# A gated recurrence and an MLP on one core: Strassen products in float32 replaced by three products of 12-bit halves

## The chip, the core and the metric

The kernel runs on one core of a Trainium2 chip. The metric is the device time of one execution in microseconds (us). All inputs come from device memory and the result goes back there.

## What is computed

The inputs q, k, v and alpha are float32 with 4 batches, 8 heads, 768 positions and 48 features a head. The weights are stored as 64-bit floats.

```python
for t in range(S):
    state = alpha[:, :, t, :, None] * state + np.einsum('bhd,bhe->bhde', k[:, :, t], v[:, :, t])
    y[:, :, t] = np.einsum('bhd,bhde->bhe', q[:, :, t], state)
x = y.transpose(0, 2, 1, 3).reshape(B, S, H * D)          # 4 x 768 x 384
mu = mean(x); var = mean((x - mu) ** 2)
xn = (x - mu) / sqrt(var + 1e-06) * g_ln
out = x + maximum(xn @ w_ch1, 0.0) @ w_ch2                # 384 -> 1536 -> 384
```

## The kernel before

The 768 positions are cut into 6 chunks of 128, so there are 24 blocks (chunk c, batch b) of 128 tokens. `attention(c, b)` (L298) takes one block from its loads to the normalised x, transposed for the MLP: logarithm of alpha and running sums (L317, L320, L407), scaled k and q (L327, L329), their transposition on TensorE in chunks 0 and 1 (L355) and by DVE and DMA from chunk 2 on (L366, L372, L379), masked scores (L397 in chunk 0, L405 later, L411 and L417), the state (L432, L441, L445, and the multiplication by the gates on POOL, L447), the outputs (L458, L463, L467), x, its mean and variance (L493, L496, L513), xn (L519, L523) and its transposition, on TensorE in chunks 0 to 3 (L530, L532), by DVE and DMA in chunks 4 and 5 (L536, L540, L543). From chunk 4 on (`split`, L387) the scores of the last head pair go to another buffer.

The weights come in 12 pieces of 768 KB, six of w_ch1 and six of w_ch2. `round_weights` (L209) turns each from 64-bit to float32 with integer operations on DVE (L219, L221, L223, L229), one activation (L227) and a multiplication on DVE (L233 with the gain g_ln, or L236).

The MLP of chunk 0 is plain: 12 hidden tiles of 128 for each half of the batches (`hidden`, L567 on TensorE, L570 on ACT), then 12 products a block (`project`, L579). From chunk 1 on it is made of fast matrix products in the manner of Strassen. The first layer is cut 3 x 3 x 2 and takes 15 products in place of 18 (`hidden_product`, L842, matmul in L857, 4 tiles of 128 x 256 a product and chunk). The sums that go into them are made on DVE (`combine_first`, L786, once; `combine_x`, L814, per chunk), and the results are put together on DVE, ACT and POOL (L865 to L900). `relus` (L903) rectifies in place. The second layer is cut 4 x 3 x 2 and takes 20 products in place of 24 (`product`, L676, matmul in L683, 4 matmuls of 128 x 192 a product and chunk), with sums by `combine_weights` (L625) and `combine_hidden` (L654, L670) and results by L693, L696 and, on POOL, L699.

PSUM has 6 banks under the tag "bank" and two for the state. All operands are float32.

Nothing reorders the work: every part is a Python generator, and the string `ORDER` says, letter by letter, whose next step is recorded. Each engine runs its instructions in that order and waits for semaphores. All transfers are issued from SyncE (SP), one queue.

Of the kernel before, what the change touches and what calls it, by code (L numbers as in the profile page):

```python
# [14 lines left out]
INT64 = mybir.dt.int64  # L15
AFT = mybir.ActivationFunctionType
AOP = mybir.AluOpType
# [4 lines left out]
X_BY_DMA = 4  # L22
SPLIT = 4
AHEAD = 2
G = 32
SCORES = ((0, 0), (0, 1), (1, 0), (1, 1), (3, 0), (2, 0), (3, 1), (2, 1))

ORDER = (
    "bacabcadaacbcaadbcadabcababbebaccbadbaaBbccaedcbceAeeaaacbfecfBcdafddeaedbdeafae"
    "bcdccbfgadhAdcgCcdbebeebfhggdfgbfffbCdcgfgecdfchgdfhgabcddchdhAiiegjhacehedhhjfg"
    "biAdfidAeBhBijffYYiCjZZYYifZYlZCgjYDlYYjjZZYBZYgDieEgDgDjZZekEhZYGZgZigZGeeYgYgg"
    "fZYEhfGfkChihiYFYijfgEhgkhFZYhgYfghijgkFeZZlGZShfZYHlhHfYFYZeZHelYiZgllPmZkJIgJk"
    "PeiYjJIflHeSZIQgkIlYSjiPkffennSQlOKjLSnSjmSQhKnSjLnKPkiljnhSQnLkkjkWknkShOmPhkhl"
    "kOOhWlmmphmQmkmXjWQnXjlSQjPmkilXSXkP2OXWjXQjkjW2iXoSWX2oWX22Pi2mnol1j1mom2omSpoo"
    "l1XSpk2oW2m112p1m2pm11m1W211pp12O122r22jnn21lpnmnjSml1riOn2l12Rl111kqS1m21W1Rkp2"  # L40
    "o21mUXpq1mU2rUrnmj1rl2Rno2oomqonrormpokO1rNM2Mipin1op1ionoqUM2qp2W12RkMmNqiMoRtk"
    "UrpkqNM1NoMliMlNUMMNMNMKNqMlNorMWrnmtltNRMsqppMWNMriMMMpNlsqqqnoqttNttMtMsXMMssM"
    "sMNMNMX1oXXppMvstM2MXMMNMsppXoMXoqMsMMXM1nqqv11Xq1trMq2tqX21rn12v1r2ur2r222rvsqs"
    "svsu1rs1nuvvt2s11ss11p22rtsvosn2uropuXru222221uts212stnU1211u1121222Op1Rp2tRU21R"
    "Us1pXqU11x2tO2MM1vwMUM12xuRvu1vurNNNNwtOuuMwRxvNtxRNutwwMM2MOwNXwMNuXMMtNM1rMMMw"
    "qtXMMMxNUNxtMMsNMMMxXxMtXtrMMqMNrMXNvutMMwNuMMMNMMMxMLMOM11vvuq2X2O2wMus1wX11222"
    "2r2Xt1222w22utsqxvw2x2ww1vx21sX12121xwvq2O2x2w111u1uvU121w12s1wuRvx12U11J1q21R1U"
    "OvRxU121wMMu2xxsRNMw2NNMRM1MUNN2MMuUMqXN1MrNNRMNvMXNXMMMM2MMMxNM1uNXMMNMNMOXMXMv"
    "MMXOMMMXxNxwxMMvNMMMMMXMx21w1x222212v12w222x122w2212X11UX2212121121121wx111MU11X"
    "2RR2v1211212211R1URU211XOUM2XNRX1MX1RM2MXN2MXNXNMXXMXMMMN111U1MN1M1122MNM1MM2MM1"  # L50
    "11NNN121O11NM1MM21N1112N1122M1MMM12MM12N222M22M2RM1M2N22MM2MU1ON2M22M2UURR22RNNM"
    "MNM1MMOMRMNMUUM2ONMNNNMO2MMMUMNMMMMMRMMNNMMMNMNMMNMMMMMMMMNMNMMMMMMM"
# [4 lines left out]
def kernel(  # L57
# [17 lines left out]

# [10 lines left out]
    NJ = DF // P  # L104
    assert S % P == 0 and H % 2 == 0 and D <= 64 and DM % P == 0 and DF % P == 0
# [3 lines left out]
    raw = ctx.enter_context(tc.tile_pool(name="raw", bufs=B // 2))  # L109
    stage = ctx.enter_context(tc.tile_pool(name="stage", bufs=STAGED))  # L110
# [4 lines left out]

    nc.scalar.preload_act_table_set("natural_log_exp_and_others")

    HS = P // 2
    halves = [slice(HS * s, HS * s + HS) for s in range(2)]

    raws = {}

    def load(c, m, names):

        bs = range(2 * m, 2 * m + 2)
        rows = slice(c * P, (c + 1) * P)
        for n, src in (("a", alpha), ("k", k), ("q", q)):
            if n in names:
                t = raw.tile([P, 2, 2, NP, D], FP32, name=f"r{n}", tag="in", bufs=7)
                step = 1 if n == "a" and c == 0 else 2  # L130
                for i in range(0, 2, step):
                    nc.sync.dma_start(  # L132
                        t[:, i:i + step].rearrange("t b i p d -> t b (i p d)"),
                        src[bs.start + i:bs.start + i + step, rows].rearrange("b t h d -> t b (h d)"))
                raws.update({(n, c, b): t[:, b - bs.start] for b in bs})
        if "v" in names:
            vn = raw.tile([P, 2, 2, NP, D], FP32, name="vn", tag="vn")
            nc.sync.dma_start(vn.rearrange("t b i p d -> t b (i p d)"),
                              v[bs.start:bs.stop, rows].rearrange("b t h d -> t b (h d)"))
            vx = None  # L140
            if c:


                vx = raw.tile([P, 2, NP, D], FP32, name="vx", tag="vx")
                src = v[bs.start:bs.stop, rows].rearrange("b (s t) h d -> s t b (h d)", s=2)
                parts = ((0, 0, NP, NP), (1, 0, NP, 0))
                if c >= SPLIT:
                    parts = ((0, 0, NP, NP - 1), (1, 0, NP - 1, 0), (1, NP - 1, 1, H - 1))
                for h, to, n, at in parts:
                    nc.sync.dma_start(  # L150
                        vx[halves[h]].rearrange("t b p d -> t b (p d)")[:, :, to * D:(to + n) * D],
                        src[1 - h, :, :, at * D:(at + n) * D])
            for b in bs:
                raws["v", c, b] = vn[:, b - bs.start], vx[:, b - bs.start] if c else None

    lone = {}

    def load_one(n):

        c, b = divmod(n, B)  # L160
        for n, src in (("a", alpha), ("k", k), ("q", q)):
            if n not in lone:
                lone[n] = raw.tile([P, 2, 2, NP, D], FP32, name=f"r{n}", tag="in", bufs=7)
            t = raws[n, c, b] = lone[n][:, b % 2]
            rows = src[b, c * P:(c + 1) * P]
            nc.sync.dma_start(t.rearrange("t i p d -> t (i p d)"),
                              rows.rearrange("t h d -> t (h d)"))
# [11 lines left out]
    for m in range(B // 2):  # L179
        load(0, m, "a")  # L180

    w1 = cpool.tile([P, NJ // 2, NF, 2 * P], FP32, name="w1")
    w2 = cpool.tile([P, NJ, DM], FP32, name="w2")
    small = cpool.tile([P, 2 * NF + 3], FP32, name="small")
    g_col, eps, least = small[:, :NF], small[:, NF:NF + 1], small[:, NF + 1:NF + 2]
    g_part, zero_col = small[:, NF + 2:2 * NF + 2], small[:, 2 * NF + 2:]
# [3 lines left out]
    pieces = []  # L190
    for i in range(NJ // 2):
        cs, js = slice(2 * i * P, 2 * (i + 1) * P), slice(2 * i, 2 * (i + 1))
        pieces.append((w1[:, i], w1_src[:, :, cs]))
        pieces.append((w2[:, js], w2_src[:, js]))
    pieces = pieces[::2] + pieces[1::2]
    staged = {}

    def load_weights(i):
        if i >= len(pieces):
            return  # L200
        dst, src = pieces[i]
        if src.dtype != FP32:
            dst = staged[i] = stage.tile(list(dst.shape), INT64, name="ws", tag="ws")
        nc.sync.dma_start(dst, src)
        if i == 0:
            with nc.allow_non_contiguous_dma(reason="one small column load"):
                nc.sync.dma_start(g_col, g_ln.rearrange("(f p) -> p f", p=P))

    def round_weights(i):  # L209

        dst, _ = pieces[i]
        ws = staged.pop(i)
# [9 lines left out]
        if i == 0:  # L225
            nc.scalar.mul(g_part, g_col, 2.0 ** -20)
# [12 lines left out]
    def take_weights(i):  # L239
        if i < STAGED:  # L240
            load_weights(i)
            yield
# [726 lines left out]
```

## Time and profile before

| | us |
|---|---|
| time, median of 3 runs (lowest to highest) | 421.62 (420.76 to 421.73) |
| span of the profiled execution, first to last instruction | 418.9 |
| TensorE (PE) busy | 409.0 |
| VectorE (DVE) busy | 351.4 |
| ScalarE (ACT) busy | 178.0 |
| GpSimd (POOL) busy | 153.2 |

The profiled execution has no time of its own beside its span; what lies around the span is taken as the difference to the median, 2.7 us. In the profile PE stands for matmuls and PEld for weight loads, which overlap them. L12 is line 12 of the kernel; a group names what is written and what is read (out<-in) and its shape. A matmul's record includes the way through the array, so records that follow each other overlap, and their spacing is read from the chain of waits, where each piece is counted from the end of the one before.

### The profile page before, as it was taken

The page shows a single profiled execution, that of the slowest core. Times are in us where ns is not written, and L with a number is a line of the kernel's source. Part 1 is how long each engine was busy: PE and PEld are TensorE (multiplying, and loading weights), DVE is VectorE, ACT ScalarE, POOL GpSimd, SP SyncE. Part 2 cuts the span into 40 slices and gives each one's busy share as a digit, 9 for nine tenths or more (in the row PEclk, how much of TensorE's full clock was granted, in tenths as well). Part 3 has the DMA queues.
Part 4 walks back from the last instruction along what each step waited for, and adds up shares of the span by engine and source line. Part 5 has one row for each costly group of instructions (what it writes and reads, how often), then busy time and mean ns, then how long its engine had stood idle before and what let it go on. Part 6 is the DMA issues. An engine that isn't in the chain of part 4 may idle for free.

```text
span 418.9 us, 11553 instructions
## 1 busy us (share of the span) xinstructions
PE 409.0 (98%) x4608; PEld 360.9 (86%) x4608; DVE 351.4 (84%) x713; ACT 178.0 (42%) x440; POOL 153.2 (37%) x169
## 2 busy tenths in 40 slices
PE   6998999999999999999999999999999999999996
PEld 4787888766678889998889999889998899999996
DVE  3999999999999989996888996688876767977873
ACT  5498456724243496414546612364313242014110
POOL 3011000003203990043395033493152940499123
PEclk9999999999999999999999999999999999999999
DMA  7998889987778778587784546433035200001201
GB/s 247 325 297 246 206 201 293 287 194 181 145 221 176 200 167 185 128 195 178 146 215 70 130 105 166 88 95 77 0 114 104 67 1 2 0 20 38 94 20 56
DMA packets 133741, 59.52 MB, mean 142 GB/s; under 512 B 90764, under 2 KB 129804, under 8 KB 133688
## 3 DMA queue, kind: packets, MB, share of 16 engines
q1 hardware_dynamic: 133688, 58.79, 55.1%
q8 instruction: 36, 0.59, 0.6%
q14 instruction: 17, 0.14, 0.1%
HBM read 42.17 MB, written 16.61 MB: 140 GB/s over the span
## 4 chain that ended last, share of the span: by engine, by line
PE 89%; DVE 4%; ACT 2%; DMA 2%; issue 1%; SPq 1%; POOL 0%; POOLq 0%; DVEq 0%
PE hps L857 31%; PE ops L683 30%; PE ops L579 8%; PE hps L567 8%; PE aps L405 3%; PE yps L463 3%; PE yps L467 2%; PE sums L432 2%; DMA rq<-in_q_dram 2%; PE xps L530 1%; PE tps L355 1%; PE aps L397 1%; PE lps L407 1%; SPq L132 1%; DVE w L221 0%
## 5 line engine op out<-in xcount | busy, mean ns | idle before, releaser
L699 POOL TENSOR_TENSOR ob<-ob,u 128x192 f32<-128x192 f32 x40 | 26.3, 668 | 64.5 <-DVE ob L696 48.3
L857 PE MATMUL hps<-sum,w 128*128 128x256 f32 x192 | 46.3, 381 | 0.0
L907 ACT ACTIVATE hT<-hT 128x512 f32<-128x512 f32 x48 | 28.8, 624 | 34.9 <-POOL hT L879 18.5
L447 POOL TENSOR_TENSOR mid<-mid,gate 112x192 f32<-112x192 f32 x20 | 11.4, 568 | 80.0 <-DVE mid L445 33.3
L683 PE MATMUL ops<-w,hT 128*128 128x192 f32 x224 | 40.5, 327 | 0.0
L857 PEld LDWEIGHTS hps<-sum,w 128*128 128x128 f32 x192 | 36.1, 190 | 5.0
L683 PEld LDWEIGHTS ops<-w,hT 128*128 128x128 f32 x224 | 37.1, 190 | 0.7 <-issue 0.2
L857 PE MATMUL hps<-xT,w 128*128 128x256 f32 x136 | 34.0, 380 | 0.0
L579 PE MATMUL ops<-w,hT 128*128 128x384 f32 x96 | 33.0, 491 | 0.0
L567 PE MATMUL hps<-xT,w 128*128 128x256 f32 x144 | 32.5, 382 | 0.0
L567 PEld LDWEIGHTS hps<-xT,w 128*128 128x128 f32 x144 | 27.0, 190 | 4.2
L683 PE MATMUL ops<-ws,sum 128*128 128x192 f32 x160 | 28.7, 327 | 0.0
L857 PEld LDWEIGHTS hps<-xT,w 128*128 128x128 f32 x136 | 25.5, 190 | 3.1
L683 PEld LDWEIGHTS ops<-ws,sum 128*128 128x128 f32 x160 | 26.5, 190 | 0.3
L579 PEld LDWEIGHTS ops<-w,hT 128*128 128x128 f32 x96 | 17.6, 190 | 10.7 <-DVE w L236 0.3
L693 DVE TENSOR_TENSOR ob<-ops,ob 128x192 f32<-128x192 f32 x50 | 17.3, 353 | 10.6 <-PE ops L683 6.5
L447 POOL TENSOR_TENSOR st<-st,gate 112x192 f32<-112x192 f32 x16 | 11.7, 729 | 37.3 <-DVE st L445 25.9
L683 PE MATMUL ops<-ws,hT 128*128 128x192 f32 x128 | 23.6, 328 | 0.0
L463 PEld LDWEIGHTS yps<-st,qT 48*64 48x64 f32 x320 | 19.9, 134 | 4.0 <-issue 2.0
L467 PE MATMUL yps<-vx,at 64*64 64x48 f32 x320 | 22.7, 219 | 0.0
L463 PE MATMUL yps<-st,qT 48*64 48x48 f32 x320 | 22.0, 220 | 0.6 <-ACT x L493 0.6
L405 PEld LDWEIGHTS aps<-qT,kT 48*64 48x64 f32 x576 | 19.0, 134 | 4.1 <-issue 0.8
(255 smaller groups left out, 1134.2 us busy)
## 6 DMA issues: line engine op xcount, KB each, us to landing
ws<-in_moe_w_ch_dram SPq DMA_DIRECT2D x12, 768.0 KB, 5.9
td<-tr SPq DMA_DIRECT2D x64, 96.0 KB, 3.1
vn<-in_v_dram SPq DMA_DIRECT2D x12, 384.0 KB, 4.3
kept<-x SPq DMA_DIRECT2D x20, 192.0 KB, 3.0
ob<-kept SPq DMA_DIRECT2D x20, 192.0 KB, 3.1
out_dram<-ob SPq DMA_DIRECT2D x19, 192.0 KB, 1.9
ra<-in_alpha_dram SPq DMA_DIRECT2D x16, 192.0 KB, 2.6
kT<-td SPq DMA_DIRECT2D x32, 96.0 KB, 4.2
```

What stands on the lines that cost most here:

```text
L405: nc.tensor.matmul(to, kT[rs, p, s], qT[rs, p, s], start=True, stop=True)
L432: nc.tensor.matmul(up[h, p], qk_of(c, b)[ts, 1, p, i, :h.stop - h.start], vn[ts, i, p], start=True, stop=True)
L447: nc.gpsimd.tensor_mul(new, new, by)
L463: nc.tensor.matmul(yps[i][halves[s], i, p], qT[rs, p, s], (now, mid)[s][rs, p], start=True, stop=r != i)
L467: nc.tensor.matmul(yps[r][halves[s], i, p], at[halves[r], p, s], by, start=r != i, stop=True)
L567: nc.tensor.matmul(hps, w1[:, j // 2, f, j % 2 * P:][:, :P], xT_of[0][:, f, bs], start=(f == 0), stop=(f == NF - 1))
L579: nc.tensor.matmul(ops_of[b], hT_of[c][:, j, b], w2[:, j], start=(j == 0), stop=(j == NJ - 1))
L683: nc.tensor.matmul(acc, lhs[:, j], rhs[:, j], start=(j == 0), stop=(j == NT - 1))
L693: nc.vector.tensor_add(x, acc, x)
L699: getattr(nc.gpsimd, f"tensor_{op}")(x, x, y)
L857: nc.tensor.matmul(acc[:, i], w, b, start=True, stop=True)
L907: nc.scalar.activation(out=x, in_=x, func=AFT.Relu)
```

## The change

In place of the fast products, the MLP from chunk 1 on splits each operand into a high and a low part of 12 bits: h = round((1 - 2^-13) w), l = w - h. With d = h - 2^12 l on the weights' side and 2^-12 h - l on the other, three products give the whole: a sum of h h and l l in one accumulation, times (1 + 2^-12), minus the product of the differences. All operands of these matmuls are float32r. Chunk 0 keeps its float32 products.

- **Weights.** `take_weights` scales on ACT and multiplies on POOL what L233 and L236 did on DVE. `split_weights` makes three tiles a piece: two activations on ACT, two subtractions on POOL.
- **x.** All chunks are transposed on TensorE. Two activations (ACT), a subtraction on DVE and one on POOL make the three parts, per block.
- **First layer.** For each half-chunk (two batches) and each two hidden tiles: 6 matmuls for the difference, 12 for the sum, 256 columns each, in two banks. Then a copy (ACT), a scaled sum (DVE), two rectified copies (ACT), the low part (DVE) and the difference (POOL). The middle of this chain has two buffers, the hidden tiles have one set for all half-chunks.
- **Second layer.** Per block 12 matmuls of 384 columns for j 0 to 5, 12 for j 6 to 11, 12 for the difference; two DVE operations add them to x.
- **Loads** of alpha, k, q and v are by block. The number of DMAs is 397, before 390.
- **ORDER** is new throughout.

The added functions, cut to their core (numbers on the left are the changed kernel's lines):

```diff
+    # take_weights, after the integer operations (175 to 185)
+            act(out=lo, in_=lo, func=AFT.Relu, scale=8.0, bias=least)
+                for f in range(NF):
+                    act(out=dst[:, f], in_=dst[:, f], func=AFT.Copy, scale=g_part[:, f:f + 1])
+            stt(out=hi, in0=hi, scalar=-(1 << 31), in1=lo, op0=AOP.bitwise_and,
+                op1=AOP.bitwise_or)
+            nc.gpsimd.tensor_mul(dst, dst, hi.bitcast(FP32))
+    def split_weights(i):                                            # 192 to 200
+        whole, _, high, low, diff = pieces[i]
+        act(out=rd(high), in_=whole, func=AFT.Copy, scale=1 - LOW / 2)
+        nc.gpsimd.tensor_sub(rd(low), whole, high)
+        act(out=rd(low), in_=low, func=AFT.Copy, scale=1 / LOW)
+        nc.gpsimd.tensor_sub(rd(diff), high, low)
...
+        act(out=rd(xh), in_=xps, func=AFT.Copy, scale=1 - LOW / 2)   # 460 to 465, attention
+        act(out=rd(xs), in_=xps, func=AFT.Copy, scale=LOW * (1 - LOW / 2))
+        nc.vector.tensor_sub(rd(xl), xps, xh)
+        nc.gpsimd.tensor_sub(rd(xs), xs, xl)
...
+    def first_products():                                            # 520 and 526
+        for m in PAIRS:
+            for t in range(NT):
+                for i in range(2):
+                    for f in range(NF):
+                        nc.tensor.matmul(b[:, i], rd(wj[i * NF + f][2]), rd(xv[f][2]),
+                                         start=(f == 0), stop=(f == NF - 1))
+                yield
+                for i in range(2):
+                    for f in range(NF):
+                        for e in range(2):
+                            nc.tensor.matmul(a[:, i], rd(wj[i * NF + f][e]), rd(xv[f][e]),
+                                             start=(f == 0 and e == 0),
+                                             stop=(f == NF - 1 and e == 1))
+    # the hidden step, in five generators (540 to 570)
+                act(out=z_of(t), in_=acc_of.pop(("b", m, t)), func=AFT.Copy, scale=-1.0)
+                stt(out=z_of(t), in0=acc_of.pop(("a", m, t)), scalar=1 + LOW, in1=z_of(t),
+                    op0=AOP.mult, op1=AOP.add)
+                act(out=rd(high), in_=z_of(t), func=AFT.Relu, scale=1 - LOW / 2)
+                act(out=rd(diff), in_=z_of(t), func=AFT.Relu, scale=LOW * (1 - LOW / 2))
+                stt(out=rd(low), in0=z_of(t), scalar=0.0, in1=high, op0=AOP.max,
+                    op1=AOP.subtract)
+                nc.gpsimd.tensor_sub(rd(diff), diff, low)
+    def second_products():                                           # 586
+                    js = range(NJ) if part == 2 else range(part * NT, part * NT + NT)
+                    for j in js:
+                        of = pieces[NT + j // 2][2:]
+                        for k, x in ((2, hs),) if part == 2 else ((0, hh), (1, hl)):
+                            nc.tensor.matmul(a, rd(x[:, j, i]), rd(of[k][:, j % 2]),
+                                             start=j == 0 and k != 1, stop=j == NJ - 1 and k != 0)
+    def results():                                                   # 595 and 598
+                stt(out=ob, in0=acc_of.pop(("a", c, b)), scalar=1 + LOW, in1=ob,
+                    op0=AOP.mult, op1=AOP.add)
+                nc.vector.tensor_sub(ob, ob, acc_of.pop(("b", c, b)))
+                send(c, b)
-    combine_weights, combine_hidden, product, combine_first, combine_x, hidden_product, relus
```

More of the change, by code (lines that the diff above doesn't have):

```diff
@@ L15 @@
 INT64 = mybir.dt.int64
+F32R = mybir.dt.float32r
 AFT = mybir.ActivationFunctionType
@@ L118 @@
     HS = P // 2
     halves = [slice(HS * s, HS * s + HS) for s in range(2)]
[L121 to L154, printed above, removed]
@@ L178, with at_first @@
         nc.gpsimd.tensor_copy(out=consts[h, 2 * P:], in_=tri[h, h])
[L179 to L183, printed above, removed]
+    def at_first(name, then):
+        return [cpool.tile([P, then[0] * then[1]], FP32, name=n, tag=name, bufs=1)
+                for n in ("early_" + name, name)]
+    w1h, w1l = (cpool.tile([P, NT, NF, 2 * P], FP32, name=n) for n in ("w1h", "w1l"))
+    early, w2h = at_first("w2h", (NJ, DM))
```

861 lines of the change are left out of this document (295 added, 566 removed).

## The prediction

> **What bounds the kernel now.** I read the page first: its totals, its slices and the chain.
>
> ```profile
> span 418.9 us, 11553 instructions
> ...
> PE 409.0 (98%) x4608; PEld 360.9 (86%) x4608; DVE 351.4 (84%) x713; ACT 178.0 (42%) x440; POOL 153.2 (37%) x169
> ...
> PE   6998999999999999999999999999999999999996
> ...
> DVE  3999999999999989996888996688876767977873
> ...
> PEclk9999999999999999999999999999999999999999
> ...
> PE 89%; DVE 4%; ACT 2%; DMA 2%; issue 1%; SPq 1%; POOL 0%; POOLq 0%; DVEq 0%
> PE hps L857 31%; PE ops L683 30%; PE ops L579 8%; PE hps L567 8%; PE aps L405 3%; PE yps L463 3%; PE yps L467 2%; PE sums L432 2%; DMA rq<-in_q_dram 2%; PE xps L530 1%; PE tps L355 1%; PE aps L397 1%; PE lps L407 1%; SPq L132 1%; DVE w L221 0%
> ```
>
> PE is busy in every slice but the first and the last, its clock is full throughout, and 61% of the chain is the two Strassen products (L857, L683). A busy PE is not yet a PE at its peak, so I asked for its work by stage, and for the chain in order of time, where back-to-back records show their true spacing.
>
> ```profile
> 0.00:40.00 40.00, 34.04 (x573) 27.90 (x574) 32.23 (x72) 28.39 (x73) 6.40 (x15) 1.00 0.96 286
> 40.00:410.00 370.00, 369.28 (x4003) 327.57 (x4002) 316.15 (x635) 149.26 (x367) 143.89 (x149) 1.00 0.52 128
> 410.00:419.00 9.00, 5.68 (x35) 5.38 (x34) 2.99 (x7) 0.32 (x1) 2.87 (x5) 1.00 0.19 66
> ```
> ```profile
> 39.75 11.85 PE hps L567 x54
> ...
> 80.59 2.58 PE ops L579 x8
> ...
> 84.47 0.33 PE xps L530 x3
> ...
> 300.61 13.00 PE ops L683 x80
> 313.61 24.17 PE hps L857 x112
> ```
>
> (The columns of the first are PE, PEld, DVE, ACT and POOL busy.) From 40 to 410 us PE is never free, and no other engine is as full. A record of 256 columns takes 24.17/112 = 0.2158 us, one of 192 columns 13.00/80 = 0.1625, one of 384 columns 2.58/8 = 0.3225: all are 0.833 ns a column and 2.5 ns. So the price of the MLP is columns times records, and the change is read on PE.
>
> **The change, part by part.** A float32 product is two records here:
>
> ```profile
> L567 PE MATMUL hps<-xT,w 128*128 128x256 f32 x144 | 32.5, 382 | 0.0
> ...
> L857 PEld LDWEIGHTS hps<-xT,w 128*128 128x128 f32 x136 | 25.5, 190 | 3.1
> ...
> L530 PEld LDWEIGHTS xps<-consts,xn 128*128 128x128 f32 x48 | 5.7, 141 | 3.1 <-ACT small L226 1.8 <-issue 0.4
> ```
>
> L567 stands for 24 tiles of 3 products, 72, and has 144 records. *Removed:* L857 makes 15 products x 4 tiles x 5 chunks = 300 matmuls, 600 records, x 0.2158 = 129.5 us; L683 makes 20 x 4 x 5 = 400, 800 records, x 0.1625 = 130.0 us. Together 259.5 us.
>
> *Added:* 10 half-chunks x 12 tiles x 3 blocks x 3 terms = 1080 matmuls of 256 columns, and 20 token blocks x 12 x 3 = 720 of 384 columns. Both are 276,480 columns. No row shows a float32r matmul. From above it costs what a record costs now, 0.2158 and 0.3225 us; the transposes, one record each, also take 0.33/3 = 0.110 us for 128 columns. From below it costs half the stream: 256 x 0.4167 + 2.5 = 109.2 ns and 162.5 ns. I take the lower end: two records are needed now because one operand comes in two parts, and by the same arithmetic the other part of each record's time goes to the two parts of the other operand; with both cut to 12 bits neither is left. Then the sum is 1080 x 0.1092 + 720 x 0.1625 = 117.9 + 117.0 = 234.9 us, **24.6 us less** than 259.5. The upper end gives 465.3 us, 205.8 more.
>
> The Trainium skill ("FP8 and Floating Point Precision", TensorE Precision Notes) says the same of the passes: true FP32 is four, and a reduced FP32 reads four bytes and truncates to FP22. By that sentence the sum is the lower end; no run so far shows it.
>
> The weights must be hidden as well. A load of 128 float32 columns is modelled at 190 ns, and the transposes' at 141; the 215.8 ns cycle of L857 hides it. At 109 ns there is less room. The nearest row with a load and a stream of equal length is the score product of chunk 0, in two row groups that run beside each other:
>
> ```profile
> L397 PE MATMUL aps<-qT,kT 48*128 48x128 f32 x18 | 1.4, 291 | 0.0
> ```
>
> These are the records that start between 12.6 and 13.6 us: 9 in each group, one per 111 ns, for a stream of 128 x 0.833 = 107 ns. So a load as long as the stream adds some 2.5 ns, 2.7 us over 1080 records. I count nothing for it and keep 2.7 for the range. The margin is narrow: 24.6 us over 1800 records is **13.7 ns a record**.
>
> *Chunks 4 and 5 of x* were turned by DVE and DMA (L536, L540, L543) and now go through PE: 8 x 3 transposes x 0.110 = **+2.6 us**. Attention's other PE work stays in number: scores, sums and outputs only lose the special case of the last head pair (L387).
>
> *DVE* loses the Strassen sums, and *ACT and POOL* gain:
>
> ```profile
> L907 ACT ACTIVATE hT<-hT 128x512 f32<-128x512 f32 x48 | 28.8, 624 | 34.9 <-POOL hT L879 18.5 <-POOL hT L895 8.2 <-DVE hT L889 4.4
> ...
> L873 ACT COPY u<-hps 128x512 f32<-128x512 f32 x8 | 4.7, 584 | 12.9 <-PE hps L857 9.9 <-issue 3.1
> ```
> ```profile
> L869 DVE TENSOR_TENSOR hT<-hps,hT 128x512 f32<-128x512 f32 x8 | 5.5, 689 | 1.9 <-PE hps L857 1.7
> ```
> ```profile
> L883 POOL TENSOR_TENSOR hT<-hT 128x512 f32<-128x512 f32 x8 | 11.1, 1391 | 0.6
> ...
> L879 POOL TENSOR_TENSOR hT<-hT,u 128x512 f32<-128x512 f32 x8 | 10.2, 1280 | 6.3 <-DVE hT L878 6.2
> ```
>
> Each of 60 hidden steps (two tiles of 256 columns) needs on ACT one copy from PSUM and two rectifiers, 0.58 + 2 x 0.62 = 1.8 us; on DVE two passes, 1.4 us; on POOL one subtraction, 1.3 to 1.4 us. PE has 18 x 0.109 + 12 x 0.1625 = 3.9 us of work for the same step, and more with attention. Averaged over the MLP these engines are under half full, so I cost this chain at nothing, hidden behind the other products and attention, with two exceptions.
>
> (1) **The splitting of the weights.** POOL gains for each of 12 pieces one product and two subtractions of 768 columns; 768/512 of 1.28 us is 1.9 us. The built order on POOL puts, between the first hidden subtraction and the point where the last three pieces of w2 have their low halves, 3 hidden steps more and 10 weight subtractions, with four small operations of attention: 4 x 1.3 + 10 x 1.9 + 3.3 = 27.5 us, and up to the last difference one hidden step and 2 weight subtractions more, 33 us in all. On PE the same stretch holds the rest of the first half-chunk, part of the next one, attention and the first two parts of a w2 product, 28 us. That leaves 33 - 28 = **+5.0 us** of PE waiting. On ACT this stretch has 8 x 1.8 us of hidden steps, 12 scalings of the weights and attention's share, some 34 us, so it ends no earlier. Nothing on PE stands behind it but the same products, which wait with it; lower bound 0, if PE comes there late for other reasons, upper bound 15, if all of ACT's excess adds.
>
> (2) **The last half-chunk**, when attention is over. The low half of its last tiles comes after DVE 0.7, ACT 1.2, DVE 0.7 and four hand-overs, 3 us; one part of a w2 product, 12 x 0.1625 = 1.95 us, can run meanwhile. **+1.3 us.** The end after the last matmul stays:
>
> ```profile
> 414.22 1.46 PE L683 MATMUL ops<-w,at 128*128 128x192 f32 x8
> ...
> 415.96 0.36 DVE L693 TENSOR_TENSOR ob<-ops,ob 128x192 f32<-128x192 f32 x1 [1.12 <-POOL ob L699]
> ```
>
> PE ends at 415.7 now, 3.2 us before the end of the span; afterwards it is one DVE pass (0.56 for 384 columns) and one DMA again.
>
> *Start.* The first w1 matmul stands at 39.75 us with DVE full until then. In the new order less of chunk 1 comes before it, so it should start about 8 us earlier, but with about 9 us less of PE work done: no gain, give or take 4. *SP* has 397 transfers for 390: 40 go with the turning of x, and the loads are cut by batch. DMA is 52% full in the long stage, so I count nothing; what waits behind a late transfer on SP is the next load of the same kind, one block ahead.
>
> *Sum:* 418.9 - 24.6 + 2.6 + 5.0 + 1.3 = 403.2 us of span. The median of the runs is 421.6, 2.7 above this span: 403.2 + 2.7 = **405.9 us**.
>
> **The rivals.**
> *Clean:* the order hides the splitting, and the start gains 4: 405.9 - 5.0 - 1.3 - 4 = 395.6 (391 to 397). For it: PE is full for 370 us today with DVE at 85%, so an order can hide a near-full engine. Against: POOL and ACT both exceed PE in one stretch. 0.12.
> *Starved:* the five-engine chain of a hidden step (PE, ACT, DVE, ACT, DVE, POOL) has two buffers for its middle, and every half-chunk must wait until the one before has read the hidden tiles. One exposed hand-over of 1 to 2 us in each of 10 half-chunks, and the 15 us in the stretch above, give 413 to 435. It ends slower than before from 16 us of waiting beyond my 6.3. For it: 60 such chains are new; against: twice the time on PE for each. 0.20.
> *A dear record, slower:* the single-pass record isn't half the old one. It decides from (24.6 - 2.6 - 5.0 - 1.3)/1800 = 8.7 ns a record. At the transposes' 0.86 ns a column the time is 405.9 + 465.3 - 234.9 = 636 us; if only the weights' load binds the 256-column ones at 150 ns, 405.9 + 1080 x 0.041 = 450 us. For it: every float32 row streams at 0.83; against: the operands' halves. Here the change would not do what it says. 0.11.
> *Loads not hidden at all:* each full-array record pays its load of some 107 ns (as in L397) ahead of its stream: 405.9 + 1800 x 0.107 = 599 us. In L857 this is excluded: 0.2158 us is the stream alone. 0.02. The Trainium skill ("TensorE: Matmul & The Clock Gate", Part 3, The mechanism) states that LDWEIGHTS overlaps matmuls in flight only when the row group differs, which speaks for this rival; L857, all on full rows, disagrees by 107 ns a record.
>
> **How the numbers follow.** Forecast 405.9, its own range 397 to 413, 0.55; clean 0.12; starved 0.20; dear record 0.11; unhidden loads 0.02. A measurement can tell about 0.3%, 1.3 us, from no change. Starved lies for 0.08 below 420.3, 0.03 within, 0.09 above. Faster: 0.55 + 0.12 + 0.08 = 0.75; same 0.03; slower 0.09 + 0.13 = 0.22. For 8 in 10, the range takes the forecast, two thirds of clean and most of starved: 393 to 428.
>
> **What would show it.** Records of the w1 products 109 to 112 ns apart and of the w2 products 162 to 163; 1800 of them; PE waiting for POOL or ACT between the first w1 product of chunk 1 and its first w2 product, 4 to 8 us, and little after. Wrong: a spacing above 118 ns; PE free for over 1 us in most half-chunks; a first w1 matmul after 36 us.

## The result, and the profile after

The changed kernel takes **444.25 us** (median of 4 runs, 442.81 to 444.90) against 421.19 (420.45 to 421.73) of the kernel before on the same chip: 1.0555 times, 95% interval 1.0528 to 1.0582. The forecast was 405.9 us, with a range of 393 to 428. The profiled execution has a span of 442.6 us, 23.7 more than before.

The page of the changed kernel: totals, slices and chain.

```profile
span 442.6 us, 12334 instructions
...
PE 415.9 (94%) x5032; PEld 377.9 (85%) x5032; DVE 280.8 (63%) x428; ACT 261.9 (59%) x578; POOL 198.8 (45%) x165
...
PE   7799796999995899999799999999999999999996
...
POOL 2043645675469961731711905334518326153170
PEclk9989899599998699999999999999999999999999
...
PE 82%; DVE 8%; ACT 4%; issue 2%; DMA 2%; SPq 1%; POOL 1%; DVEq 0%
```

PE now has holes, all but one in the first 14 slices (to 155 us), and beside them its granted clock is down. The same by stretches (columns as in the prediction: PE, PEld, DVE, ACT, POOL busy, then the clock):

```profile
40.00:80.00 40.00, 33.31 (x359) 26.87 (x359) 35.51 (x35) 27.62 (x61) 22.05 (x14) 0.91 0.55 165
80.00:120.00 40.00, 40.00 (x284) 25.50 (x283) 22.60 (x29) 18.64 (x41) 24.06 (x17) 0.92 0.46 128
120.00:160.00 40.00, 32.26 (x426) 30.69 (x425) 28.76 (x33) 29.45 (x56) 34.41 (x22) 0.87 0.43 98
160.00:442.00 282.00, 276.17 (x3598) 267.04 (x3596) 161.98 (x273) 158.17 (x354) 109.45 (x100) 1.00 0.47 116
```

From 160 us on PE is full again at full clock. Its four longest waits, from the view of waits (the first three end before 160 us, the fourth lies at 211 us):

```profile
PE hpb L520 <- POOL xs L465: 7.0, 1, 7.0
PE hps L483 <- DVE at L366: 3.5, 1, 3.5
PE hps L483 <- DVE early_w2h L293: 2.5, 1, 2.5
PE opa L586 <- DVE at L546: 2.4, 1, 2.4
```

A second finding is in the chain in order of time, in stretches where nothing waits:

```profile
152.84 0.68 PE hpb L520 x6
153.52 1.36 PE hpa L526 x12
...
161.00 2.08 PE opb L586 x12
163.08 2.08 PE opa L586 x12
```

A record of 256 columns takes 1.36/12 = 0.1133 us, one of 384 columns 2.08/12 = 0.1733; I had put 109.2 and 162.5 ns. That alone is 1080 x 4.1 + 720 x 10.8 ns = 12.3 us.

To see where PE's time went I gave each record the time to the next record's start, took out waits over 0.3 us, and summed by line:

| PE, us | before | after | difference |
|---|---|---|---|
| MLP products of chunks 1 to 5 | 263.0 | 259.0 | -4.0 |
| MLP products of chunk 0 | 63.7 | 67.8 | +4.1 |
| attention and transposes | 81.0 | 86.9 | +5.9 |
| waits over 0.3 us | 6.6 | 23.8 | +17.2 |
| first to last record | 414.2 | 437.6 | +23.4 |

(The lines are rounded, and add up to 23.2.)

Of 24.6 us that the products should have saved, 4.0 arrived; and PE waits 17.2 us more. The two lines that hold most of it are different questions, so I split the time at one point, the first w2 product of chunk 1, from the view of its line:

```profile
L586 PE MATMUL opa<-w2h,hid x240: 333/334/446, 156.6 to 436.5; 128*128 128x384 f32 x120
...
L586 PE MATMUL opb<-ws,hid x240: 331/334/423, 160.8 to 438.7; 128*128 128x384 f32 x120
```

**The start stretch is 156.6 us, the rest 438.7 - 156.6 = 282.1 us**, and only 3.2 us of the waits lie in the rest. Below, these two figures are those of each run's profiled execution, not medians.

Why DVE is named in the waits can be read from its groups, of the kernel before and of the changed one (mean ns after the comma):

```profile
L221 DVE SCALAR_TENSOR_TENSOR w<-ws,w 128x768 f32<-128x768 uint32 x12 | 11.5, 959 | 0.4
...
L329 DVE TENSOR_TENSOR qk<-rq,eq 128x384 f32<-128x384 f32 x20 | 11.4, 569 | 0.4 <-DMA rq<-in_q_dram 0.4
```
```profile
L546 DVE SCALAR_TENSOR_TENSOR at<-hpa,at 128x512 f32<-128x512 f32 x60 | 40.9, 687 | 31.9 <-PE hpa L526 24.7 <-ACT at L540 3.8 <-ACT lps L287 1.3
L169 DVE SCALAR_TENSOR_TENSOR w<-early_w2l,w 128x768 f32<-128x768 uint32 x12 | 23.1, 1924 | 0.4
L295 DVE TENSOR_TENSOR qk<-qk,eq 128x384 f32<-128x384 f32 x16 | 18.8, 1176 | 0.0
...
L171 DVE TENSOR_SCALAR early_w2l<-early_w2l 128x768 int32<-128x768 int32 x12 | 10.4, 868 | 0.4
```

The first two of the kernel before take twice as long in the changed one (L221, now L169: 959 to 1924 ns; L329, now L295: 569 to 1176), while L546, which reads PSUM, has 687. L171, with one input from SBUF, has 868 here and 578 in run 1 below, where POOL has less to do. The timeline ahead of the 7.0 us wait, of POOL and of DVE, shows how:

```profile
134.76 1.86 POOL L200 TENSOR_TENSOR ws<-w2h,w2l 128x768 fp32r<-128x768 f32 x1
136.57 0.51 POOL L417 TENSOR_TENSOR st<-st,gate 112x192 f32<-112x192 f32 x1
137.03 1.84 POOL L196 TENSOR_TENSOR w2l<-w,w2h 128x768 fp32r<-128x768 f32 x1
138.83 3.58 POOL L200 TENSOR_TENSOR ws<-w2h,w2l 128x768 fp32r<-128x768 f32 x2
```
```profile
135.05 7.77 DVE L295 TENSOR_TENSOR qk<-qk,eq 128x384 f32<-128x384 f32 x1
142.74 0.55 DVE L463 TENSOR_TENSOR xl<-xps,xh 128x384 fp32r<-128x384 f32 x1
```

L295 with its two SBUF inputs stands for 7.77 us, until POOL's run of subtractions ends at 142.4; L463 is queued behind it, and POOL's L465 and PE's hpb behind that. The Trainium skill ("SBUF — State Buffer", SBUF: two separate sides) calls the shared port pair of DVE and GpSimd an exclusive lock, held for a whole instruction; the trace agrees and is harsher, since DVE didn't get in between five instructions.

### The profile page after: what moved, and what is told of

Read it like the earlier page. It is cut to its first block, busy times and chain, and to the rows that moved or that the text cites. A ratio compares the mean times of both kernels' runs of the same rounds, so it can differ in the third digit from the quotient of the medians.

```text
span 442.6 us, 12334 instructions
## 1 busy us (share of the span) xinstructions
PE 415.9 (94%) x5032; PEld 377.9 (85%) x5032; DVE 280.8 (63%) x428; ACT 261.9 (59%) x578; POOL 198.8 (45%) x165
## 4 chain that ended last, share of the span: by engine, by line
PE 82%; DVE 8%; ACT 4%; issue 2%; DMA 2%; SPq 1%; POOL 1%; DVEq 0%
PE opa L586 19%; PE hpa L526 19%; PE hpb L520 10%; PE opb L586 9%; PE ops L495 8%; PE aps L354 4%; PE yps L408 3%; PE hps L483 3%; DVE w L169 2%; PE yps L411 2%; PE sums L380 2%; PE xps L449 2%; DMA early_w2l<-in_moe_w_ch_dram 2%; PE lps L211 1%; DVE qk L295 1%
## 5 line engine op out<-in xcount | busy, mean ns | idle before, releaser
L570 POOL TENSOR_TENSOR hid<-hid 128x512 fp32r<-128x512 f32 x60 | 83.9, 1414 | 51.4 <-ACT hid L555 19.6
L526 PE MATMUL hpa<-xh,w1h 128*128 128x256 f32 x360 | 87.0, 282 | 0.0
L526 PE MATMUL hpa<-xl,w1l 128*128 128x256 f32 x360 | 86.2, 279 | 0.0
L586 PE MATMUL opa<-w2h,hid 128*128 128x384 f32 x240 | 82.5, 344 | 2.4 <-DVE at L546 2.4
L586 PE MATMUL opa<-w2l,hid 128*128 128x384 f32 x240 | 80.5, 336 | 0.5 <-DVE hid L562 0.5
L526 PEld LDWEIGHTS hpa<-xh,w1h 128*128 128x128 f32 x360 | 68.8, 191 | 0.3
L526 PEld LDWEIGHTS hpa<-xl,w1l 128*128 128x128 f32 x360 | 68.7, 191 | 0.0
L546 DVE SCALAR_TENSOR_TENSOR at<-hpa,at 128x512 f32<-128x512 f32 x60 | 40.9, 687 | 31.9 <-PE hpa L526 24.7
L520 PE MATMUL hpb<-xs,ws 128*128 128x256 f32 x360 | 54.1, 287 | 7.0 <-POOL xs L465 7.0
L562 DVE SCALAR_TENSOR_TENSOR hid<-at,hid 128x512 fp32r<-128x512 f32 x60 | 55.3, 940 | 8.0 <-ACT hid L554 6.8
L185 POOL TENSOR_TENSOR w<-w,early_w2l 128x768 f32<-128x768 f32 x12 | 22.9, 1908 | 50.6 <-DVE early_w2l L182 32.1
L554 ACT ACTIVATE hid<-at 128x512 fp32r<-128x512 f32 x60 | 37.6, 626 | 7.7 <-DVE at L546 7.5
L555 ACT ACTIVATE hid<-at 128x512 fp32r<-128x512 f32 x60 | 37.2, 620 | 3.8 <-PE opb L586 3.8
```

Of the source, the lines that this page charges most:

```text
L185: nc.gpsimd.tensor_mul(dst, dst, hi.bitcast(FP32))
L520: nc.tensor.matmul(b[:, i], rd(wj[i * NF + f][2]), rd(xv[f][2]), start=(f == 0), stop=(f == NF - 1))
L526: nc.tensor.matmul(a[:, i], rd(wj[i * NF + f][e]), rd(xv[f][e]), start=(f == 0 and e == 0), stop=(f == NF - 1 and e == 1))
L546: stt(out=z_of(t), in0=acc_of.pop(("a", m, t)), scalar=1 + LOW, in1=z_of(t), op0=AOP.mult, op1=AOP.add)
L554: act(out=rd(high), in_=z_of(t), func=AFT.Relu, scale=1 - LOW / 2)
L555: act(out=rd(diff), in_=z_of(t), func=AFT.Relu, scale=LOW * (1 - LOW / 2))
```

## Theories and experiments

Three theories for the start stretch, as the expectations below name them. *Port:* POOL's work on the weights holds DVE, which means that DVE's instructions stand while POOL's run. *Queue:* POOL has too much to do, and PE waits for its results; in a wider form, the work is too much for the in-order engines, whichever does it. *Order:* the last instructions ahead of a waiting product stand badly. Beside them: the record's price, and the lowered clock.

**1. POOL's 36 operations on the weights left out.**

```
-            nc.gpsimd.tensor_mul(dst, dst, hi.bitcast(FP32))
...
-        nc.gpsimd.tensor_sub(rd(low), whole, high)
...
-        act(out=rd(low), in_=low, func=AFT.Copy, scale=1 / LOW)
+        act(out=rd(low), in_=whole, func=AFT.Copy, scale=1 / LOW)
...
-        nc.gpsimd.tensor_sub(rd(diff), high, low)
```

> Left out: POOL's three operations on each piece of the weights (36 of 768 columns, some 69 us of POOL). The weights stay unscaled, the low part is a scaled copy of the whole, the high part stands in for the difference; every matmul, DMA, DVE and ACT instruction stays. Port theory (a DVE instruction that reads two tensors from SBUF stands still while POOL reads; it stood 35.8 us in the first 160 us of the changed kernel): the holds before 160 us fall below 5 us, PE's idle time there falls by 25 to 30 us, time 414 to 420. Queue theory (POOL has too much to do, and PE waits for its results): the same time here, so this run only separates these two from the third. Order theory (the new order and its latencies, the late weights and ACT's load cost the time, whatever POOL does): 437 to 444.

428.09 us, 1.0184 (1.0167 to 1.0201): 16 us back, and 8 us above the kernel before (420.21 beside this run) remain. That is 8 us more than port and queue expected and 9 less than order did, so POOL's work on the weights accounts for 16 us, which isn't all of the loss. The start stretch is 141.0 us, the rest 282.4, unchanged:

```profile
L583 PE MATMUL opa<-w2h,hid x240: 333/334/446, 141.0 to 421.1; 128*128 128x384 f32 x120
```

**2. The same operations as POOL memsets, three for one** (each writes the tile and reads nothing).

```
-        nc.gpsimd.tensor_sub(rd(low), whole, high)
+        nc.gpsimd.memset(low, 1.0)
...
```

> Left out: the content of the same 36 operations. Each is replaced by three memsets of the tile that it wrote, so that POOL stays about as long busy (3 x 0.72 = 2.1 us for 1.9) and all waits stay, but POOL reads nothing there. Port theory: DVE is no longer held (below 8 us before 160 us for 35.8), time 415 to 425. Queue theory: POOL is as late as before, time 440 to 448. Order theory: 437 to 448.

441.11 us, 1.0498 (1.0458 to 1.0539). The hold of the two-input instructions is gone (L169 is back at 960 ns), though POOL is busier than before (212.8 us). The one-input L171 is still held, with 900 ns for 578 in run 1:

```profile
L169 DVE SCALAR_TENSOR_TENSOR w<-early_w2l,w 128x768 f32<-128x768 uint32 x12 | 11.5, 960 | 0.4
L182 DVE SCALAR_TENSOR_TENSOR early_w2l<-early_w2l 128x768 int32<-128x768 int32 x12 | 11.5, 956 | 7.8 <-ACT early_w2l L175 7.8
L171 DVE TENSOR_SCALAR early_w2l<-early_w2l 128x768 int32<-128x768 int32 x12 | 10.8, 900 | 0.4
```

The start stretch falls to 148.9 us, half of what leaving the work out gives, but the median falls by 3 us only. The rest was 285.0 in this execution. One part of that has nothing to do with the edit: some 50 us into the rest PE waits for 2.4 to 2.6 us in most runs, and in some traces (runs 2, 3, 6, 7, 9 and 10) 3.4 us at half clock follow, in others (the changed kernel, runs 1, 8, 11 and 12) none. So differences of 1 to 2 us in the rest say nothing. Queue and order had expected the time, port 415 to 425.

**3. The operations on DVE** (nothing left out).

```
-        nc.gpsimd.tensor_sub(rd(low), whole, high)
+        nc.vector.tensor_sub(rd(low), whole, high)
...
```

> The same 36 operations go to DVE, nothing is left out. DVE gets 36 x 0.96 = 35 us of work and POOL loses 69 us. Port theory: what DVE gets equals what it loses in holds before 160 us, and POOL's latency (1.9 us for 0.96) goes: time 420 to 434. Queue theory: POOL is free, so 415 to 425. Order theory, with DVE now 35 us fuller: 444 or more.

442.53 us, 1.0535 (1.0503 to 1.0567); start stretch 151.2 us, rest 283.9. L169 takes 1031 ns. The port theory alone falls: with none of the weights' work on POOL the kernel is still 22 us slower than the one before. The queue theory's number (415 to 425) falls with it: a free POOL doesn't help when DVE has the work. Of it the wider form is left, and order's 444 or more is as near.

**4. The differences of x and of the hidden tiles on DVE,** the weights still on POOL.

```
-        act(out=rd(xs), in_=xps, func=AFT.Copy, scale=LOW * (1 - LOW / 2))
-        nc.gpsimd.tensor_sub(rd(xs), xs, xl)
+        stt(out=rd(xs), in0=xh, scalar=LOW, in1=xl, op0=AOP.mult, op1=AOP.subtract)
...
-                nc.gpsimd.tensor_sub(rd(diff), diff, low)
+                stt(out=rd(diff), in0=high, scalar=LOW, in1=low, op0=AOP.mult, op1=AOP.subtract)
```

> The differences of x and of the hidden tiles are made by one DVE operation each (high x 2^-12 - low) in place of an ACT copy and a POOL subtraction; weights stay on POOL; nothing is left out. DVE gets 60 x 0.69 + 20 x 0.55 = 52 us, ACT loses 47 us, POOL 105 us. Port theory: the holds of the second DVE operation of a hidden step (15.4 us in all) go, but most of them lie after 160 us where PE has other work, and those before 160 us come from the weights: time 436 to 444. Queue theory: POOL's weight work is through earlier by some 12 us in the stretch before the first w2 product: 430 to 438. Order theory: 437 to 444, with less ACT work perhaps 435.

448.60 us, 1.0679 (1.0663 to 1.0695): above what all three theories expected, with a start stretch of 161.5 us and a rest of 281.4. Relieving ACT and POOL at DVE's cost makes the start longer and the rest no shorter.

**5. The record by itself.** PE alone, series of 24 on their own lines:

```
+    for i in range(24):
+        nc.tensor.matmul(acc[0][:, :384], rd(w[:, i % 6 * P:][:, :P]), rd(x[:, :384]), ...)
```

> This kernel leaves out the whole computation: PE alone makes series of 24 matmuls in float32r of 128, 256, 320, 384 and 512 columns, then in bfloat16 of 256, 384 and 512, each with a new load, and float32r of 384 columns once more with the same weights each time; no other engine works beside it. In the changed kernel the records stood 113.3 ns (256 columns) and 173.3 ns (384) apart, not 109.2 and 162.5. Theory 'the record is like that': alone on the chip the spacing is again 113 and 173, so 0.469 ns a column less 6.7 (128: 53, 320: 143, 512: 233) or about 0.445 ns a column (512: 227). Rival 'neighbours slow it': reads of SBUF by the other engines or by the loads cost it 4 and 11 ns; alone it is 109 and 162.5, 512 columns 216, and the series with the same weights is the faster one. bfloat16 should show 109, 162 and 216 under both.

The chain: L82 is float32r of 256 columns, L88 of 384, L91 of 512, L94, L97 and L100 the bfloat16 ones, L103 384 columns with the same weights.

```profile
43.04 2.87 PE acc L82 x24
...
70.14 4.17 PE acc L88 x24
...
84.67 5.48 PE acc L91 x24
...
100.51 2.62 PE acc L94 x24
...
113.49 3.90 PE acc L97 x24
...
143.29 4.18 PE acc L103 x24
```

Float32r: 119.6 ns, 173.8, 228.3; bfloat16: 109.2 and 162.5. With no neighbours the float32r record is as dear or dearer, 0.445 to 0.47 ns a column, and at 384 columns it is no cheaper with the weights kept (174.2 for 173.8). The series with kept weights has no counterpart at 256 columns. The 128-column series, expected at 53 ns, stood at 108, so a record that short is set by something other than its columns; no run shows by what.

**6, 7. A second set of x buffers, and x's last turns moved forward** (on top of run 1).

```
-            pair_of[pair] = [work.tile([P, NF, HB, P], FP32, name=f"x{i}", tag=f"x{i}", bufs=1)
+        if pair not in pair_of and pair[1]:
+            pair_of[pair] = [cpool.tile([P, 2, DM], FP32, name=f"x{i}", tag="whole", bufs=2 * NT)
...
-    "...)21.113.*++hh)23iiii)hh*kh1111kkkh..hhhh++hhh445gggg*lmk..."
+    "...)21.1gggg13.*++hh)23iiii)hh*kh1hhh11hhhh1kkkh..++445*lmk..."
```

> As the run without POOL's work on the weights (which leaves out their 36 operations and took 428.1), with a second set of buffers for the split x, used by every odd half-chunk, and the order as it was. What is left of PE's waiting there is one wait of 5.1 us ahead of the second half-chunk, for POOL's difference of x, followed by 6.8 us at half clock. Buffer theory: the split of x can't start before the last w1 product of the half-chunk before it, because of its one buffer: the wait shrinks by 3 us or more, 422 to 425. Order theory: the transposes of this x stand behind that product on PE anyway, so a buffer alone changes nothing: 427.5 to 429. Queue theory (ACT, DVE and POOL are late whatever the place): the same 427.5 to 429.

> As the kernel with two sets of x buffers, and the last turns of the third and fourth token block of chunk 1 (transposes of x, its split) moved ahead: one block before the last four w1 products of the half-chunk before, the other before its last one. Order theory (with the buffers as its condition): the wait of 5.1 us goes to under 1.5 and the half clock after it goes, 6.8/2 = 3.4 us more: 428.1 - 4 - 3 = 421 (419 to 423). Queue theory: what is late is the work of ACT, DVE and POOL itself; the wait moves to the next product, 425 to 428.

432.15 us, 1.0269 (1.0236 to 1.0302), and 433.13, 1.0277 (1.023 to 1.0323). The start stretch is 139.8 and 141.4 us, as in run 1 (141.0): neither the buffer nor the order shortens it, and both theories fall. With x early, PE's 5.3 us of waiting became 1.5 + 1.4 + 2.9 us at three places; the chain shows ACT in them, with the scaling of the weights in its queue:

```profile
124.61 0.71 ACT xn L442
...
127.60 1.48 ACT w2l L196 x2
129.08 0.52 ACT hid L555
129.60 0.52 ACT hid L556
```

Both are 4 to 5 us slower than run 1, with a rest of 286.8 us for 282.4. The larger part goes with the buffer that x is read from. Two pieces of run 6's chain, from the fifth half-chunk (x in the old buffers) and from the sixth (x in the new set):

```profile
252.48 1.36 PE hpa L527 x12
...
280.53 1.44 PE hpa L527 x12
```

These are 113.3 and 120 ns a record. In both runs it is so throughout: records of half-chunks that read the new set stand mostly 120 ns apart, the others 113 to 118, with the same weights. From chunk 2 on that is 4 x 108 x 6.7 ns = 2.9 us; the spell at half clock named in run 2 is in both traces too. What about the place of x makes the difference isn't shown.

**8. PE kept busy in its waits** by products of two constants.

```
+        for n in (10, 15, 30):
+            for _ in range(n):
+                nc.tensor.matmul(warm, ident, tri, start=True, stop=True)
+            yield
...
```

> The changed kernel, nothing left out, with useless products of two constants on PE in front of three of its waits (10 ahead of the eleventh w1 tile of chunk 0, 15 ahead of its 23rd, 30 ahead of the second half-chunk of chunk 1; 0.22 us each at full clock, 2.2, 3.3 and 6.5 us against waits of 2.6, 3.7 and 7.2). Clock theory: the granted clock fell to 0.5 after each of these waits, for 3.4, 10.2 and 10.2 us, and PE loses half of what of this it is busy; with PE kept busy the clock stays at 1.0 there and the time falls by (3.4 + 9.2 + 5.9)/2 = 9 us: 435 (432 to 438). Rival 'the clock costs nothing there': PE waits for other engines in this stretch anyway, so work done sooner only waits longer: 443 to 446. If the clock doesn't answer to idle time, it falls at the same places and the time is 444 or more.

443.30 us, 1.053 (1.0499 to 1.0561). Waits and what follows them, in the changed kernel and in this one:

```profile
73.80:86.70 12.90, 9.36 (x80) 6.50 (x80) 12.37 (x12) 7.26 (x16) 7.58 (x4) 0.60 0.28 92
138.60:151.60 13.00, 5.99 (x29) 5.85 (x28) 11.33 (x10) 10.62 (x21) 12.04 (x9) 0.61 0.38 79
```
```profile
73.80:86.70 12.90, 11.81 (x119) 8.79 (x118) 12.38 (x14) 7.15 (x16) 7.59 (x5) 1.00 0.28 93
138.60:151.60 13.00, 12.63 (x112) 12.44 (x111) 11.35 (x11) 10.06 (x20) 12.04 (x8) 1.00 0.34 68
```

The clock went from 0.60 to 1.00, and the time fell by 1 us (start stretch 153.3, rest 284.1). My clock theory was wrong: PE gets its work done sooner, then waits longer for the same engines (new waits of 1.8 us at 105.8 and 1.4 at 159.3). That the clock answers to idle time is shown: with PE kept busy in these three waits the half clock behind them is gone; the Trainium skill ("TensorE: Matmul & The Clock Gate", Part 1, What's actually happening) states half rate after an idle window of about 3.4 us. The traces agree for long waits (4.8 to 9.1 us, always followed by half clock); of waits of 2.1 to 2.6 us some were followed by it (2.45 in the changed kernel, at 45 us) and some not (2.38, at 211 us).

**9. A cheaper record in place:** PE reads only the upper half-word of each split operand.

```
+    def top(x):
+        return x.bitcast(mybir.dt.bfloat16)[:, 1::2]
...
-                            nc.tensor.matmul(a, rd(x[:, j, i]), rd(of[k][:, j % 2]),
+                            nc.tensor.matmul(a, top(x[:, j, i]), top(of[k][:, j % 2]),
```

> The changed kernel with one edit: PE reads of each split operand of the MLP only the upper 16 bits, as bfloat16 (every second half-word), so that it leaves the lower half out of the products; all other engines do the same work. Alone on the chip bfloat16 records stood 109 ns (256 columns) and 162.5 ns (384) apart, float32r ones 116 to 120 and 173. Theory 'record price': after the first w2 product of chunk 1 (at 156.6 us) PE sets the time, so the cheaper record comes through: 912 x (116.3 - 109.2) + 720 x (180 - 162.5 - 4) = 6.5 + 9.7, a time of 428 to 433, and the stretch before it hardly changes. Rival 'the other engines bind': ACT, DVE or POOL set the pace of the hidden steps all along, the records are shorter and PE waits instead: 440 to 444.

438.75 us, 1.0402 (1.0363 to 1.0440), between the two ranges and short of what I expected, because bfloat16 at every second half-word stood at 113 and 169 ns (12 records in 1.36 and 2.03 us), not 109 and 162.5. As far as the record is cheaper, it comes through: start stretch 155.8, rest 277.8, which is 4.3 us less, where the w2 records alone give 720 x 4.3 ns = 3.1. PE binds the rest.

**10, 11. Run 1 by halves:** only w1's 18 operations left out, only w2's.

```
+        if i >= NT:        # the other run: if i < NT
             nc.gpsimd.tensor_sub(rd(low), whole, high)
...
```

> The changed kernel without POOL's 18 operations on the weights w1 (the product, the low half, the difference of six pieces; the low half is then scaled from the whole, the high half stands in for the difference); those on w2 stay. Without all 36 the time was 428.1, and the first w2 product of chunk 1 came at 141.0 instead of 156.6 us. Theory 'work ahead of the chain': the 18 on w1 stand between 40 and 120 us, where attention of chunk 1 and chunk 0 wait for DVE and POOL; without them the first w1 product of chunk 1 comes at 105 to 109 instead of 116.8 us, and the time is 434 to 437. Rival 'the last wait alone': what counts is only the halves of w2 and x right ahead of the first w2 product; without w1's the time is 441 to 444.

> The counterpart: POOL's 18 operations on w2 left out in the same manner, those on w1 kept. By 'work ahead of the chain' the first w1 product stays within 4 us of 116.8 and the stretch from it to the first w2 product falls from 39.8 to 34 to 37 us: 436 to 440. By 'the last wait alone' nearly the whole of the 16 us comes back: 428 to 432. If the two runs together bring back clearly more or less than 16 us, the parts aren't separate.

432.12 us, 1.0265 (1.0219 to 1.0311), and 442.18, 1.0469 (1.0410 to 1.0529). The first w1 product of chunk 1, in the changed kernel, without w1's operations and without w2's:

```profile
L520 PE MATMUL hpb<-xs,ws x360: 275/276/582, 116.8 to 424.9; 128*128 128x256 f32 x180
```
```profile
L523 PE MATMUL hpb<-xs,w1h x360: 275/276/581, 103.6 to 412.7; 128*128 128x256 f32 x180
```
```profile
L523 PE MATMUL hpb<-xs,ws x360: 275/276/582, 116.4 to 422.5; 128*128 128x256 f32 x180
```

w1's work costs 13.2 us, before chunk 1's products have begun; the stretch with the long wait, where I had looked for it, gives back 2 to 3 with w2's. The theory "work ahead of the chain" had the place right and the size too small for w1 (434 to 437) and too large for w2 (436 to 440); its rival falls with both. The start stretches are 142.4 and 153.6 us, so the two parts give 14.2 and 3.0 where run 1 gave 15.6: they are separate to within 2 us.

**12. Both suspects out:** runs 1 and 9 in one.

> Both suspects taken out at once: the kernel without POOL's 36 operations on the weights (428.1), and PE reads only the upper 16 bits of the split operands. If the start stretch (until the first w2 product of chunk 1) and the price of a record after it are two separate terms, they add: 428.1 - 14 = 414 (411 to 417), below the kernel before. If with the cheaper record the hidden steps of ACT, DVE and POOL bind, it is 420 to 428.

421.31 us, 1.0017 (0.9993 to 1.0042), start stretch 138.5, rest 276.3. 16.2 and 5.5 us apart, 22.9 together: the two terms add. My number missed by what the record in run 9 had not become cheaper. The time lies in the range of the rival, but the trace doesn't bear the rival out: in the rest PE waits only twice for more than 0.6 us, 3.4 us in all.

**13, 14. Plain halves.** High x high, low x high and high x low in one bank need no differences.

```
-        nc.gpsimd.tensor_sub(rd(diff), high, low)
...
+                        for w, x in ((wh, xh), (wl, xh), (wh, xl)):
+                            nc.tensor.matmul(a[:, i], rd(w), rd(x), ...)
```

> The three single passes in another form, with the same 1800 records in float32r: high x high, low x high and high x low are summed in one PSUM bank (the product of the two low halves is left out). So the differences of the halves go: 12 subtractions on POOL and 12 scalings on ACT for the weights, for x one pass each on ACT and POOL per token block, and a hidden step is two ACT passes and one DVE pass (before: three, two and one on POOL). Theory 'work ahead of the chain': the stretch until the first w2 product of chunk 1 falls from 156.6 to 138 to 146 us; after it PE sets the time and nothing changes but the 3 us of waits, 279 to 284; time 423 to 433. Rival 'the three passes bind': attention and the chain of x set that stretch, 152 to 157, and the time is 438 to 444.

> The same with the halves kept as bfloat16, packed (8 bits each, so the products lose what is below the 16th bit of an operand). By the spacing of single runs of records (bfloat16 109.2 and 162.5 ns, float32r 116 and 173; read at every second half-word it was 113 and 169) PE has 912 x 7 + 720 x 11 = 14 us less after the first w2 product: 266 to 271 there, and a time of 408 to 419, below the kernel before. If packing doesn't matter, the records stay at 113 and 169, and it is 418 to 428. If with shorter records ACT, DVE or POOL bind, PE waits for hidden tiles in most half-chunks and the time stays at that of the float32r form.

430.81 us, 1.0219 (1.0173 to 1.0266): start stretch 146.1 and rest 279.4, so the differences, with the passes on ACT, DVE and POOL that make and use them, cost 10.5 us of the start. With packed bfloat16 halves **413.45 us, 0.9826 (0.9800 to 0.9853)**: faster than both kernels, by 1.7% than the one before, for products that lose what is below the 16th bit of an operand. From its page and its chain:

```profile
span 409.7 us, 11936 instructions
...
PE 391.0 (95%) x5032; PEld 296.2 (72%) x5032; DVE 206.6 (50%) x348; ACT 214.1 (52%) x486; POOL 72.5 (18%) x73
```
```profile
210.88 1.95 PE opa L552 x12
212.83 5.89 PE hpa L511 x54
```

Records of 0.1625 and 0.1091 us, as in run 5, and POOL at 72.5 us for 198.8. The start stretch is 141.7, the rest 264.1.

## Why the prediction was wrong, by its steps

The step that failed first is the splitting of the weights: it was counted, as +5.0 us, only from the first hidden subtraction on, and POOL's work on w1 ahead of that was put at nothing. It costs 16 us in all, 13.2 of them ahead of the first w1 product (runs 1 and 10), in a stretch where PE isn't full. The second is the record's price, which no row showed, 12.3 us. Read on PE, the forecast span of 403.2 us is missed by 39.4 us: 12.3 of price, 4.0 of products at lowered clock, 4.4 more of hand-overs, 10.9 of waits beyond the 6.3 forecast, 4.1 in chunk 0, 3.3 in attention and transposes beyond the 2.6 forecast, 0.3 around PE's records.

- **The record (109.2 and 162.5 ns) was mis-sized.** It measured 113.3 and 173.3, 12.3 us over 1800 records. I took the lower of two ends with an argument about passes that says nothing of a pass's pace; runs 5 and 14 show that this pace is bfloat16's. The mechanism was right: about half the price a column (0.833 before, 0.45 now), and no load in sight. The rival "dear record" named the point from which it decides (8.7 ns a record); the measured 6.8 on average lie short of it, so the price alone would not have turned the sign.
- **"Together 259.5 us" became 234.9 only on paper, 259.0 on PE.** Beside the 12.3, 4.0 us are the 168 records of the start stretch at lowered clock (23.0 us for 19.0 at full pace), and 7.9 in the rest are hand-overs between products and attention (236.0 for 912 x 0.1133 + 720 x 0.1733 = 228.1); the kernel before had 3.5 of such over its 259.5.
- **"The splitting of the weights, +5.0" was the right suspect in the wrong place and far too small.** I counted POOL and PE from the first hidden subtraction on. Run 11 shows 2 to 3 us there; run 10 shows 13.2 us ahead of the first w1 product at 117 us, where I had costed POOL's w1 work at nothing. That PE waits 7.0 us for POOL between the first w1 and the first w2 product of chunk 1, near the 4 to 8 that I gave as a sign, is luck: it waits for the difference of x, and 5.1 us of this wait stay when POOL has no weights to split (runs 1 and 11).
- **"DVE loses" work was true of its total (351 to 281 us) and misleading:** of the 281 at least 36 are instructions that stand while POOL reads (L169 12 x 0.965, L295 16 x 0.607, L562 60 x 0.25 against L546, which is as large). How much of the 16 us is hold and how much queue stays open: run 2, without the two-input hold, gives back 7.7 of run 1's 15.6 us by the start stretches and 3 of 16 by the medians, its POOL is 14 us busier, and its memsets still hold L171.
- **The hidden chain "at nothing"** held in the rest, where PE waits for 3.2 us in all: so the rival "starved" didn't come in every half-chunk. The 15 us that it put between the first hidden subtraction and the last w2 difference are some 8 (7.0 of them one wait); most of PE's 20.6 us of waits in the start lie ahead of that. **The differences** that three products in this form need, costed at nothing on all engines but for the weights', cost 10.5 us of the start (run 13); part of this is the weights' work of run 1.
- **Chunk 0 and attention:** transposes +2.6 as predicted (5.7 to 8.3). Chunk 0's products +4.1, from the lowered clock, weren't counted; run 8, where the clock stays up, takes 1 us less, so they cost next to nothing as long as PE waits.
- **Right:** 1800 records, loads hidden, a first w1 product of chunk 0 10 us sooner (29.5 us for 39.7) without gain, DMA without a cost (no wait of PE is put down to one), a tail that differs by under 1 us.

Open stay why a 256-column float32r record stands at 113 ns from one buffer and at 120 from another (runs 5 to 7), and what else sets the 138 to 141 us that the start takes without POOL's work. The chain of run 7 names ACT there; no run lightened ACT without loading DVE or leaving out more.

## What to carry to other kernels

Price an operand type that no row shows by a run of its own records before you multiply it by 1800, or keep both ends as equals. Split a kernel's time at the point from which PE is full: what the engines do before it can add to the time nearly one for one (run 1: 15.6 us off the start, 16.2 off the time), and work that "hides behind PE" hides only after it. When a change gives POOL long runs of SBUF reads, look at the mean durations of DVE's instructions, those with two SBUF inputs above all, not at DVE's total.

## What the runs showed of the hardware

- Float32r records: 113.3 ns for 256 columns (120 when x is read from the second set of buffers, 119.6 alone in run 5), 173.3 for 384, 228 for 512, and at 384 no faster with the weights kept; bfloat16 109.2, 162.5 and 215.8; bfloat16 at every second half-word 113 and 169. So four bytes from column to column cost about what float32r does at 256 columns, and 6.5 of its 10.8 ns at 384.
- A DVE instruction with two SBUF inputs can stand through several POOL instructions (7.77 us for 0.57); POOL's memsets don't hold it (960 ns), but do hold L171, a scalar operation with one SBUF input (900 ns for 578).
- All waits of PE of 4.8 us and more were followed by spells at half clock, of 6.8 or 10.2 us. Of those from 1.7 to 3.6 us some were, for 3.4 us and more, and some weren't.
